# ScalarE in place of VectorE for the normalised rows between two MLPs

## The chip, the core and the metric

The kernel runs on one core of a Trainium2 chip. A core has a matrix engine (TensorE, PE in the rows), a vector engine (VectorE, DVE), an engine for functions of one input (ScalarE, ACT), a general engine (GpSimd, POOL) and a queue that issues transfers (SyncE, SP). Each works through its own instructions in a fixed order and waits on semaphores for the others. The metric is the device time of one execution in microseconds, as a median over runs.

## What is computed

A decayed linear attention is followed by a token and channel MLP, then by a Fourier mixing, a normalisation of each row and a second channel MLP. The change lies in the normalisation:

```python
X = np.fft.fft(np.fft.fft(x, axis=1), axis=2)
u = x + np.real(X).astype(np.float32)
mu = np.mean(u, axis=-1, keepdims=True)
var = np.mean((u - mu) ** 2, axis=-1, keepdims=True)
un = (u - mu) / np.sqrt(var + 1e-06)
ch = np.maximum(un @ w_ch1, 0.0) @ w_ch2
return (u + ch).astype(np.float32)
```

There are two batches of 768 rows with 512 features; the first MLP has 1536 hidden features, the second 2048. Everything is float32. A product in float32 is made of three products of a rounded high part and a low part (`mm3`, L118 to L120), so each operand is split first: ACT rounds the high part and DVE or POOL subtracts it.

## The kernel before

A batch's 768 rows are six tiles of 128 rows (`u3[b][:, r, :]`, r from 0 to 5), each 128 partitions by 512 features. `fourier_rows` writes them: TensorE transposes the input into a bank `pu` (L860), DVE adds the transform (L867, L868). `norm(b, rows)` takes rows 0 to 3 at once, and later rows 4 and 5: DVE makes the statistics of each row (L882, L883), ACT the square root (L885), DVE the reciprocal with one correction step (L886 to L889, 128x4 or 128x2 numbers), and then DVE writes each normalised tile `unf_b_r`, (u - mean) * rs, with the mean and rs as one number per partition (L893). `norm_out` has TensorE transpose `unf` into a bank `pn` (L902), ACT round it (L908) and DVE subtract (L909), which makes `un`, the input of the second MLP.

This work is woven into the MLPs' own. While batch 0's rows are normalised, the first MLP of batch 1 is still running, and the transform of batch 1 begins: `fourier_ab` makes two sums `abt` at a time, one on DVE and one on POOL (L698), ACT and DVE split them into `ab` (L113, L114), and `fourier_d` multiplies them into banks `pq`.. `first` makes a block of hidden features: TensorE fills a bank `ph`, ACT makes the rounded positive part `hid` (L486), DVE the low part (L487). `second` multiplies `hid` into the accumulators `ac`. `convert` prepares one weight tile: a transfer brings the raw weights, ACT rounds them into `w_a` or `w_b` (L252), POOL subtracts (L253).

The banks `pu`, `pn`, `pq`, `pm` share two buffers (`x_bank`), so a product into one of them waits until ACT or DVE has emptied the one before the last. The tiles `unf`, `abt`, `z`, `at` share nine buffers (`temp`), the raw weights three.

A list by step numbers (`WHEN`, `TURNS`) sets the order of TensorE's and SP's instructions as the code is written. The instructions of ACT, DVE and POOL are put in order by the scheduler that builds the program; each engine's order is then fixed. In the names below, `hid_0_1_1_9` is the hidden block 9 of the first MLP, batch 1, half 1; `w_a_1_2` the weight tile 2 of the second MLP; `abt_1_0_0_1` the sum for batch 1, half 0, kind 0, made by POOL.

Of the kernel before, what the change touches and what calls it, by code (L numbers as in the profile page):

```python
# [14 lines left out]
AF = mybir.ActivationFunctionType  # L15
ALU = mybir.AluOpType
# [44 lines left out]
def body(ctx: ExitStack, tc: tile.TileContext, qkv, kT, lam, w_tok1, w_tok2,  # L61
         w_ch1, w_ch2, m_ch1, m_ch2, dft, dft_x, out, scratch, singles):
    nc = tc.nc
# [14 lines left out]
    ts = nc.vector.tensor_scalar  # L78
    stt = nc.vector.scalar_tensor_tensor
# [28 lines left out]
    def temp(w, n, dt=F32):  # L108
        return t_p.tile([P, 2 * NQ + 2], dt, tag="t", name=n)[:, :w]
# [150 lines left out]
    def convert(n=1, among=()):  # L260

        among = list(among)
        for _ in range(n):
            if at_["part"] < at_["word"] and (jobs[at_["part"]][0] == "ahead" or room(jobs[at_["part"]][1])):
                stage_part()
            if at_["word"] < at_["abs"] and at_["word"] < at_["part"] + 1:
                for op in word_ops():
                    op()
                    if among:
                        among.pop(0)()  # L270
            while at_["load"] < at_["word"] + BUFS["raw"] and len(raws) < BUFS["raw"] and load_next():
                pass
            if at_["abs"] < at_["word"] + 1:
                stage_abs()
        for op in among:
            op()
# [213 lines left out]
    u3 = {}  # L490
# [381 lines left out]
    def norm(b, rows):  # L872

        n = len(rows)
        r0 = rows[0]
        st = sm_p.tile([P, n, 6], F32, tag="bn", name=f"bn_{b}_{r0}", bufs=2)
        mv = sm_p.tile([P, n, 2], F32, tag="mv", name=f"mv_{b}_{r0}", bufs=2)
        var = sm_p.tile([P, n], F32, tag="var", name=f"var_{b}_{r0}", bufs=2)
        rs = sm_p.tile([P, n], F32, tag="rs", name=f"rs_{b}_{r0}", bufs=2)
        t1 = sm_p.tile([P, n], F32, tag="t1", name=f"t1_{b}_{r0}", bufs=2)  # L880
        for i, r in enumerate(rows):
            nc.vector.bn_stats(out=st[:, i, :], in_=u3[b][:, r, :])  # L882
            nc.vector.bn_aggr(out=mv[:, i, :], in_=st[:, i, :])  # L883
        ts(out=var, in0=mv[:, :, 1], scalar1=EPS, scalar2=None, op0=ALU.add)
        nc.scalar.activation(t1, var, AF.Sqrt)  # L885
        ops = [lambda: nc.vector.reciprocal(rs, t1),  # L886
               lambda: tt(out=t1, in0=rs, in1=rs, op=ALU.mult),
               lambda: stt(out=t1, in0=t1, scalar=-0.5, in1=var, op0=ALU.mult, op1=ALU.mult),
               lambda: stt(out=rs, in0=t1, scalar=1.5, in1=rs, op0=ALU.add, op1=ALU.mult)]  # L889
        convert(1, ops)  # L890
        for i, r in enumerate(rows):
            un = temp(DM, f"unf_{b}_{r}")
            ts(out=un, in0=u3[b][:, r, :], scalar1=mv[:, i, 0:1], scalar2=rs[:, i:i + 1],  # L893
               op0=ALU.subtract, op1=ALU.mult)
            uns[b, r] = un

    def norm_out(b, rows):
# [41 lines left out]
    for b in range(B):  # L939
        for h, (fn, *args) in zip(WHEN[b], (  # L940
                (fourier_ab, b, 0, 0), (fourier_ab, b, 0, 1), (fourier_d, b, 0, 0), (fourier_d, b, 0, 1),
                (fourier_ab, b, 1, 0), (fourier_ab, b, 1, 1), (fourier_d, b, 1, 0), (fourier_d, b, 1, 1),
                (fourier_sums, b, 0), (fourier_sums, b, 1), (fourier_y, b, 0), (fourier_y, b, 1),
                (fourier_gather, b), (fourier_columns, b, 0), (fourier_rows, b, 0), (fourier_columns, b, 1),
                (fourier_rows, b, 1), (fourier_mid, b), (fourier_columns, b, 2), (norm, b, (0, 1, 2, 3)),
                (fourier_rows, b, 2), (norm_out, b, (0, 1)), (norm_out, b, (2, 3)), (norm, b, (4, 5)),
                (norm_out, b, (4, 5)))):
            side.setdefault(h, []).append((fn, args))
# [198 lines left out]
```

## Time and profile before

| | |
|---|---|
| median of three runs | 619.23 us (619.03 to 619.75) |
| the profiled execution | 619.02 us, of which the span is 617.2 us |
| busy in the span: TensorE, VectorE, ScalarE, GpSimd | 589.6, 438.3, 235.0, 144.4 us |
| granted TensorE clock | 1.00 of 2.4 GHz throughout |

TensorE is busy nearly all the time, so the places where it waits are what is to be read. The timelines of the engines show these, each row with the idle time ahead of it and the instruction that ended it. A wait for several things is put down to the one that came last by the profile. The tables of `norm` for batch 0 lie at 301 to 323 us, those for batch 1 at 377 to 402.

### The profile page before, as it was taken

The numbers are of one execution on the slowest core, as the hardware profiler recorded it, in microseconds if no ns is written. First come the engines' busy times: TensorE is split into PE (matmuls) and PEld (weight loads), VectorE is DVE, ScalarE is ACT, GpSimd is POOL, SyncE is SP. The second block draws the span as 40 slices with busy tenths as digits, with TensorE's granted clock in tenths as the row PEclk, the third lists the DMA queues.
The fourth block names the chain that finished last, engine by engine and source line by source line (L and its number), as shares of the span: only waits on it lengthen the run. The fifth ranks groups of instructions, "written<-read, shape, count | busy, mean of one in ns | idle before, by whom it ended". The sixth has DMA issues, their size and how long they took to land. (4 is left out here: it accounts for less than half of the span.)

```text
span 617.2 us, 9630 instructions
## 1 busy us (share of the span) xinstructions
PE 589.6 (96%) x3704; PEld 545.2 (88%) x3704; DVE 438.3 (71%) x823; ACT 235.0 (38%) x480; POOL 144.4 (23%) x119
## 2 busy tenths in 40 slices
PE   8789999999999999999999999999989998999997
PEld 7777799899899999999989899878878887888896
DVE  6798998893876448638796875895798688343435
ACT  2575763532423323234454441343443333211110
POOL 5253224220400220201364110033402332300000
PEclk9999999999999999999999999999999999999999
DMA  8966335333387256100232001002405342000005
GB/s 282 406 236 225 110 102 176 103 113 110 109 268 241 69 189 219 67 1 1 60 95 70 19 1 34 18 18 81 125 0 175 116 120 87 0 1 0 1 2 204
DMA packets 24638, 65.58 MB, mean 106 GB/s; under 512 B 2824, under 2 KB 3984, under 8 KB 24592
## 3 DMA queue, kind: packets, MB, share of 16 engines
q1 hardware_dynamic: 24304, 64.83, 31.7%
q8 instruction: 29, 0.48, 0.3%
q10 hardware_dynamic: 288, 0.14, 0.1%
q14 instruction: 17, 0.14, 0.1%
HBM read 54.99 MB, written 9.97 MB: 105 GB/s over the span
## 5 line engine op out<-in xcount | busy, mean ns | idle before, releaser
L120 PE MATMUL ac<-w_b,hid 128*128 128x512 f32 x192 | 75.9, 396 | 0.3 <-DVE hid L487 0.3
L119 PE MATMUL ac<-w_b,hid 128*128 128x512 f32 x192 | 75.7, 394 | 0.0
L118 PE MATMUL ac<-w_b,hid 128*128 128x512 f32 x192 | 74.9, 390 | 0.0
L487 DVE SCALAR_TENSOR_TENSOR hid<-ph,hid 128x384 fp32r<-128x384 f32 x68 | 37.5, 551 | 50.6 <-ACT hid L486 50.6
L119 PE MATMUL ac<-hid,w_b 128*128 128x384 f32 x192 | 65.2, 339 | 2.9 <-DVE hid L487 2.7
L118 PE MATMUL ac<-hid,w_b 128*128 128x384 f32 x192 | 64.8, 337 | 0.3 <-ACT hid L486 0.3
L118 PE MATMUL ph<-uh,w_a 128*128 128x384 f32 x192 | 64.7, 337 | 0.0
L120 PE MATMUL ph<-uh,w_a 128*128 128x384 f32 x192 | 64.3, 335 | 0.0
L120 PE MATMUL ac<-hid,w_b 128*128 128x384 f32 x192 | 64.2, 335 | 0.0
L119 PE MATMUL ph<-uh,w_a 128*128 128x384 f32 x192 | 64.2, 334 | 0.0
L486 ACT ACTIVATE hid<-ph 128x384 fp32r<-128x384 f32 x68 | 33.1, 487 | 79.8 <-PE ph L120 79.8
L253 POOL TENSOR_TENSOR w_a<-m_a,w_a 128x512 fp32r<-128x512 f32 x18 | 26.2, 1454 | 104.3 <-ACT w_a L252 104.3
L120 PEld LDWEIGHTS ac<-w_b,hid 128*128 128x128 f32 x192 | 36.0, 187 | 8.4 <-DVE hid L487 0.8
L119 PEld LDWEIGHTS ac<-w_b,hid 128*128 128x128 f32 x192 | 36.0, 188 | 6.1
L118 PEld LDWEIGHTS ac<-w_b,hid 128*128 128x128 f32 x192 | 36.1, 188 | 5.8
L119 PEld LDWEIGHTS ac<-hid,w_b 128*128 128x128 f32 x192 | 36.0, 188 | 5.5 <-DVE hid L487 5.5
L253 POOL TENSOR_TENSOR w_b<-m_b,w_b 128x512 fp32r<-128x512 f32 x18 | 25.4, 1413 | 59.4 <-ACT w_b L252 44.5
L118 PEld LDWEIGHTS ac<-hid,w_b 128*128 128x128 f32 x192 | 36.1, 188 | 1.0 <-ACT hid L486 0.6
L118 PEld LDWEIGHTS ph<-uh,w_a 128*128 128x128 f32 x192 | 36.1, 188 | 0.3 <-issue 0.2
L119 PEld LDWEIGHTS ph<-uh,w_a 128*128 128x128 f32 x192 | 36.1, 188 | 0.1
L120 PEld LDWEIGHTS ac<-hid,w_b 128*128 128x128 f32 x192 | 36.0, 188 | 0.0
L120 PEld LDWEIGHTS ph<-uh,w_a 128*128 128x128 f32 x192 | 36.0, 188 | 0.0
(453 smaller groups left out, 1464.2 us busy)
## 6 DMA issues: line engine op xcount, KB each, us to landing
qkv<-qkv SPq DMA_DIRECT2D x7, 768.0 KB, 9.1
single_scratch<-m_a SPq DMA_DIRECT2D x16, 256.0 KB, 4.1
qkv<-qkv SPq DMA_DIRECT2D x10, 384.0 KB, 5.9
kp<-kT SPq DMA_DIRECT2D x8, 384.0 KB, 6.8
out<-u SPq DMA_DIRECT2D x11, 256.0 KB, 2.0
single_scratch<-m_b SPq DMA_DIRECT2D x10, 256.0 KB, 4.8
raw_t_0d<-w_tok SPq DMA_DIRECT2D x2, 384.0 KB, 9.9
raw_t_1d<-w_tok SPq DMA_DIRECT2D x2, 384.0 KB, 4.2
```

The lines of the kernel that those rows point to most:

```text
L118: nc.tensor.matmul(ps, wt[0], xt[0], start=first, stop=False, **kw)
L119: nc.tensor.matmul(ps, wt[0], xt[1], start=False, stop=False, **kw)
L120: nc.tensor.matmul(ps, wt[1], xt[0], start=False, stop=last, **kw)
L253: nc.gpsimd.tensor_tensor(out=t[:, 1, :n], in0=src, in1=f32(t[:, 0, :n]), op=ALU.subtract)
L486: nc.scalar.activation(hi, ps, AF.Relu)
L487: stt(out=lo, in0=ps, scalar=0.0, in1=f32(hi), op0=ALU.max, op1=ALU.subtract)
```

## The change

Each group gets one more small DVE instruction, t1 = -mean * rs (L890 of the new kernel). The normalised tile is then written by ACT as rs * u + t1, with rs as a scale and t1 as a bias per partition (L894); L893 on DVE is gone.

```diff
-               lambda: stt(out=rs, in0=t1, scalar=1.5, in1=rs, op0=ALU.add, op1=ALU.mult)]
+               lambda: stt(out=rs, in0=t1, scalar=1.5, in1=rs, op0=ALU.add, op1=ALU.mult),
+               lambda: stt(out=t1, in0=mv[:, :, 0], scalar=-1.0, in1=rs, op0=ALU.mult, op1=ALU.mult)]
         convert(1, ops)
         for i, r in enumerate(rows):
             un = temp(DM, f"unf_{b}_{r}")
-            ts(out=un, in0=u3[b][:, r, :], scalar1=mv[:, i, 0:1], scalar2=rs[:, i:i + 1],
-               op0=ALU.subtract, op1=ALU.mult)
+            nc.scalar.activation(un, u3[b][:, r, :], AF.Identity, scale=rs[:, i:i + 1], bias=t1[:, i:i + 1])
```

The scheduler puts other instructions into another order as well. On ACT, at rows 0 to 3 of batch 0, this stands before:

```order
L849 ACTIVATE z_0_2_3246<-at_0_2_3244 128x2x2
L252 ACTIVATE w_a_1_2_3361<-raw_a_1_2s_3281 128x512
L486 ACTIVATE hid_0_1_1_9_3275<-ph_0_1_1_9_3262 128x384
L252 ACTIVATE w_b_1_2_3368<-raw_b_1_2s_3286 128x512
L252 ACTIVATE w_a_1_3_3457<-raw_a_1_3s_3364 128x512
L908 ACTIVATE un_0_0_3335<-pn_0_0_3330 128x4x128
```

In the new program ACT has there:

```order
L849 ACTIVATE z_0_2_3246<-at_0_2_3244 128x2x2
L894 ACTIVATE unf_0_0_3311<-u3_0_3115,t1_0_0_3292,rs_0_0_3291 128x512
L894 ACTIVATE unf_0_1_3313<-u3_0_3115,t1_0_0_3292,rs_0_0_3291 128x512
L894 ACTIVATE unf_0_2_3315<-u3_0_3115,t1_0_0_3292,rs_0_0_3291 128x512
L894 ACTIVATE unf_0_3_3317<-u3_0_3115,t1_0_0_3292,rs_0_0_3291 128x512
L486 ACTIVATE hid_0_1_1_9_3275<-ph_0_1_1_9_3262 128x384
L252 ACTIVATE w_a_1_2_3362<-raw_a_1_2s_3281 128x512
L252 ACTIVATE w_b_1_2_3369<-raw_b_1_2s_3286 128x512
L252 ACTIVATE w_a_1_3_3458<-raw_a_1_3s_3365 128x512
L908 ACTIVATE un_0_0_3336<-pn_0_0_3331 128x4x128
```

The four new instructions stand behind L849, and the rounding of the weights `w_a_1_2` has moved from ahead of `hid_0_1_1_9` to behind it.

On POOL, at the same place, before:

```order
L253 TENSOR_TENSOR w_b_1_1_3303<-raw_b_1_1s_3228,w_b_1_1_3303 128x512
L253 TENSOR_TENSOR w_a_1_2_3361<-raw_a_1_2s_3281,w_a_1_2_3361 128x512
L698 TENSOR_TENSOR abt_1_0_0_1_3391<-xT_1_178 128x384
L253 TENSOR_TENSOR w_b_1_2_3368<-raw_b_1_2s_3286,w_b_1_2_3368 128x512
L253 TENSOR_TENSOR w_a_1_3_3457<-raw_a_1_3s_3364,w_a_1_3_3457 128x512
L698 TENSOR_TENSOR abt_1_0_1_1_3399<-xT_1_178 128x384
```

In the new program POOL has there:

```order
L253 TENSOR_TENSOR w_b_1_1_3303<-raw_b_1_1s_3228,w_b_1_1_3303 128x512
L698 TENSOR_TENSOR abt_1_0_0_1_3392<-xT_1_178 128x384
L253 TENSOR_TENSOR w_a_1_2_3362<-raw_a_1_2s_3281,w_a_1_2_3362 128x512
L253 TENSOR_TENSOR w_b_1_2_3369<-raw_b_1_2s_3286,w_b_1_2_3369 128x512
L253 TENSOR_TENSOR w_a_1_3_3458<-raw_a_1_3s_3365,w_a_1_3_3458 128x512
L698 TENSOR_TENSOR abt_1_0_1_1_3400<-xT_1_178 128x384
```

The first `abt` has moved ahead of `w_a_1_2`. It waits there for L849 on ACT, the last reader of the tile whose buffer it takes; before, it waited for the DVE instructions ahead.

On ACT at rows 0 to 3 of batch 1 the new program has these rows; before, the four L894 were not among them:

```order
L842 ACTIVATE at_1_2_4070<-pm_1_2_0_4056 128x258
L252 ACTIVATE w_a_1_7_4239<-raw_a_1_7s_4093 128x512
L894 ACTIVATE unf_1_0_4100<-u3_1_3862,t1_1_0_4080,rs_1_0_4079 128x512
L849 ACTIVATE z_1_2_4072<-at_1_2_4070 128x2x2
L894 ACTIVATE unf_1_1_4102<-u3_1_3862,t1_1_0_4080,rs_1_0_4079 128x512
L894 ACTIVATE unf_1_2_4104<-u3_1_3862,t1_1_0_4080,rs_1_0_4079 128x512
L894 ACTIVATE unf_1_3_4106<-u3_1_3862,t1_1_0_4080,rs_1_0_4079 128x512
L908 ACTIVATE un_1_0_4122<-pn_1_0_4117 128x4x128
```

One of them stands ahead of L849 and three behind it; all four stand ahead of L908. The orders of TensorE and SP are the same in both programs. On DVE the other instructions keep their order but for L890 and a swap of two neighbours behind rows 4 and 5 of batch 1.

## Rows read from the trace of the kernel before

**Rows 1.** Page, busy time: engine, us, share of the span, instructions.
```profile
PE 589.6 (96%) x3704; PEld 545.2 (88%) x3704; DVE 438.3 (71%) x823; ACT 235.0 (38%) x480; POOL 144.4 (23%) x119
```

**Rows 2.** Timeline of TensorE: start, length, operation, count, idle ahead and its releaser.
```profile
312.27 1.03 PE L902 MATMUL pn<-ident,unf 128*128 128x128 f32 x8
...
315.97 0.63 PE L860 MATMUL pu<-ident,g 128*128 128x128 f32 x4 [0.57 <-DVE un L909]
...
320.82 0.36 PE L118 MATMUL pq<-w_dft,ab 128*128 128x256 f32 x1 [0.77 <-DVE mv L883]
```

**Rows 3.** Timeline of DVE in the same stretch.
```profile
306.06 1.19 DVE L884 TENSOR_SCALAR var<-mv 128x4 f32<-128x4 f32 x1
...
308.42 0.16 DVE L889 SCALAR_TENSOR_TENSOR rs<-t,rs 128x4 f32<-128x4 f32 x1
308.62 4.56 DVE L893 TENSOR_SCALAR unf<-u,mv,rs 128x512 f32<-128x512 f32 x4
...
317.75 0.54 DVE L487 SCALAR_TENSOR_TENSOR hid<-ph,hid 128x384 fp32r<-128x384 f32 x1
...
318.88 0.54 DVE L114 TENSOR_TENSOR ab<-abt,ab 128x384 fp32r<-128x384 f32 x1
...
320.27 0.41 DVE L868 TENSOR_TENSOR u<-pu,z 128x256 f32<-128x256 f32 x1
```

**Rows 4.** Timeline of ACT in the same stretch.
```profile
308.00 0.21 ACT L849 ACTIVATE z<-at 128x4 f32<-128x4 f32 x1 [0.51 <-DVE rs L886]
308.31 0.63 ACT L252 ACTIVATE w_a<-raw_a_2s 128x512 fp32r<-128x512 f32 x1
310.39 0.49 ACT L486 ACTIVATE hid<-ph 128x384 fp32r<-128x384 f32 x1 [1.45 <-PE ph L120]
310.78 0.62 ACT L252 ACTIVATE w_b<-raw_b_2s 128x512 fp32r<-128x512 f32 x1
...
316.12 0.52 ACT L113 ACTIVATE ab<-abt 128x384 fp32r<-128x384 f32 x1 [0.34 <-POOL abt L698]
316.55 0.47 ACT L486 ACTIVATE hid<-ph 128x384 fp32r<-128x384 f32 x1
```

**Rows 5.** Timeline of POOL in the same stretch.
```profile
305.93 1.29 POOL L253 TENSOR_TENSOR w_b<-raw_b_1s,w_b 128x512 fp32r<-128x512 f32 x1 [2.20 <-ACT w_b L252]
309.02 1.29 POOL L253 TENSOR_TENSOR w_a<-raw_a_2s,w_a 128x512 fp32r<-128x512 f32 x1 [1.79 <-ACT w_a L252]
310.27 1.20 POOL L698 TENSOR_TENSOR abt<-xT 128x384 f32<-128x384 f32 x1
...
313.18 1.63 POOL L253 TENSOR_TENSOR w_a<-raw_a_3s,w_a 128x512 fp32r<-128x512 f32 x1 [0.28 <-ACT w_a L252]
314.77 1.32 POOL L698 TENSOR_TENSOR abt<-xT 128x384 f32<-128x384 f32 x1
317.62 1.36 POOL L253 TENSOR_TENSOR w_b<-raw_b_3s,w_b 128x512 fp32r<-128x512 f32 x1 [1.53 <-ACT w_b L252]
```

**Rows 6.** Groups of ACT instructions by form: count, busy us, mean ns, idle ahead.
```profile
L252 ACT ACTIVATE w_a<-m_a 128x512 fp32r<-128x512 f32 x18 | 11.3, 626 | 13.7 <-DVE m_a L226 12.7 <-PE h L120 0.7 <-PE ht L120 0.3
...
L401 ACT ACTIVATE qkv<-qkv,att 128x320 f32<-128x320 f32 x16 | 8.3, 553 | 13.5 <-DMA qkv<-qkv 5.4 <-DVE att L338 5.0 <-DMA att<-pw_scratch 3.0
L113 ACT ACTIVATE ab<-abt 128x384 fp32r<-128x384 f32 x16 | 7.8, 519 | 7.4 <-POOL abt L698 6.9 <-DVE abt L698 0.4
```

**Rows 7.** Timeline of TensorE at rows 0 to 3 of batch 1.
```profile
388.63 1.09 PE L902 MATMUL pn<-ident,unf 128*128 128x128 f32 x8 [0.40 <-DVE unf L893]
```

**Rows 8.** Timelines of ACT, DVE and POOL at rows 0 to 3 of batch 1.
```profile
386.19 0.63 ACT L252 ACTIVATE w_a<-raw_a_7s 128x512 fp32r<-128x512 f32 x1 [0.33 <-PE pm L120]
...
389.29 1.09 ACT L908 ACTIVATE un<-pn 128x512 fp32r<-128x512 f32 x2 [1.97 <-PE pn L902]
...
386.93 2.91 DVE L893 TENSOR_SCALAR unf<-u,mv,rs 128x512 f32<-128x512 f32 x4
...
386.90 1.29 POOL L253 TENSOR_TENSOR w_a<-raw_a_7s,w_a 128x512 fp32r<-128x512 f32 x1 [14.98 <-ACT w_a L252]
```

## The prediction

> **What bounds the kernel now.** I read the page's busy times first, then TensorE's timeline in the stretch of the normalisation, then the timelines of VectorE (DVE), ScalarE (ACT) and GpSimd (POOL) over the same stretch. TensorE is busy for 96% of the span [rows 1]: a microsecond saved elsewhere is worth something only where TensorE waits, and a microsecond added costs something only where TensorE is made to wait. Two places have such waits beside the moved lines. For batch 0, TensorE waits 0.57 us before the transposes into `pu` at 315.97 and 0.77 us before the second product into `pq` at 320.82 [rows 2]. The last is named as a wait for a DVE instruction of that moment; what it needs is the bank that L868 empties, from 320.27 for 0.41 us [rows 3], 0.14 us before TensorE goes on. For batch 1, TensorE waits 0.40 us for the normalised rows themselves at 388.63 [rows 7].
>
> The DVE instructions that the change takes away are stretched where POOL works beside them: four L893 take 4.56 us from 308.62 [rows 3], while POOL runs from 309.02 almost without a gap [rows 5]. In batch 1, with one POOL instruction beside them, four take 2.91 us [rows 8].
>
> **The change, part by part.** It takes twelve DVE instructions away, four groups of 4, 2, 4 and 2, adds one small DVE instruction (L890) to each group, and puts twelve ACT instructions (L894) into ACT's queue. The order of TensorE and of SP stays. ACT's order and POOL's order do not.
>
> *Price of one L894.* No ACT instruction of the trace has a scale and a bias per partition. With constants, 128x512 takes 0.626 us and 128x384 0.519 [rows 6], so 0.84 ns an element and 0.466 us for 320 elements. L401, with a scale per partition over 320 elements, takes 0.553 [rows 6], 0.087 more. Two such operands give 0.626 + 2 x 0.087 = 0.80 us. ACT instructions in a row start about 0.10 us before the one ahead ends (0.49 us from 310.39, the next at 310.78 [rows 4]), so one L894 each 0.71 us; the bounds are 0.53 (the operands cost nothing) and 0.80 (no overlap). I take 0.71, being worked out from the one row that has such an operand. The Trainium skill, ScalarE: Activation LUTs, in What ACT_TABLE_LOAD costs, gives 186 ns plus 0.833 ns an element plus about 93 ns for each pointer operand, by which one would take 0.80 us as well; the trace agrees for one operand, and no run here yet shows two. The functions' table is loaded once at the start in both programs.
>
> *Batch 0, rows 0 to 3.* This is where the time is decided.
>
> 1. POOL's `abt` (the input of the row transform) now stands ahead of `w_a_1_2` and waits only for L849, which ends at 308.21 [rows 4]. With the 0.08 us that POOL needs after an ACT instruction (308.94 to 309.02 [rows 4, 5]) it starts at 308.29. L889 comes on DVE at 308.42 [rows 3], reads two tiles from SBUF, and meets it. L884, as small, was held from 306.06 for 1.19 us until POOL's instruction of 305.93 had ended [rows 3, 5]. So L889 ends with POOL's 1.20 us [rows 5], at 309.5, L890 0.2 later, and the first L894 starts at 309.75. Without that meeting it would start at 308.85.
> 2. Four L894 take 4 x 0.71 = 2.84 us: `hid_0_1_1_9` starts at 312.6 instead of 310.39. In the old order `w_a_1_2` went ahead of it at 308.31; now it comes 0.39 us behind, at 313.0, ends 0.63 later at 313.6 [rows 4], and POOL begins its half at 313.7 instead of 309.02.
> 3. POOL then has four instructions before the second `abt` is there: `w_a_1_2`, `w_b_1_2`, `w_a_1_3`, `abt`. The four from 310.27 to 316.09 took 5.54 us without their one gap of 0.28 [rows 5], with DVE working against them. Alone they would take 3 x 1.25 + 1.20 = 4.95. DVE has four two-input instructions in this time again (`abt`, three L114), so I take 5.54: the second `abt` ends at 319.2 instead of 316.09.
> 4. ACT waits for that `abt` (L113 at 316.12), and `hid_0_1_1_10` stands behind it (316.55 [rows 4]); now 319.7, 3.1 us later. On DVE that tile's L487 stands ahead of L867, L868, L114, BN_STATS, L867 and L868 for the rows 4 and 5, and TensorE's second `pq` waits for the last of them. From the start of `hid_0_1_1_10` on ACT to this `pq` it is 4.27 us now [rows 2, 4]. DVE was about 0.7 us late there (L487 at 317.75 [rows 3]), which goes. In its place L114 meets POOL's `w_b_1_3`, which in the old run was nearly done (317.62 for 1.36, L114 at 318.88 [rows 3, 5]); that gives some 0.5 back. I take 4.05: `pq` starts at 323.75 instead of 320.82, **2.9 us later**.
>
> The 0.57 us at `pu` may stay or go: TensorE comes to `pq` early in both cases and waits there. The transposes of the new rows are not late: TensorE comes to them at 312.27 [rows 2], and the first L894 ends at 310.6. The raw weights that wait for POOL to free their buffers (from `raw_b_1_3` on, in SP's queue) are asked for some 5 us later; their readers on ACT stand behind the same delay, so I cost that at nothing, and at up to 1 us if one of them lands late. Bounds of the 2.9: 0.3 below (no meeting at L889, 0.53 each, POOL alone, no meeting at L114: 2.9 - 0.9 - 0.7 - 0.6 - 0.4), 4.0 above.
>
> *Batch 1, rows 0 to 3.* `w_a_1_7` starts on ACT at 386.19 [rows 8], so the first L894 at 386.7, done by 387.5; no stretch by POOL, which held L893 from 386.93 [rows 8]. TensorE finds it at 388.1 or so and saves its 0.40 us [rows 7] and some 0.2 of starting anew (an estimate: matmuls in a row overlap, and after a wait the first does not). But three more L894 and L849 stand ahead of L908, which moves from 389.29 [rows 8] to about 389.7, and the banks come free later for the next transposes: 0.3 of it remains. **0.3 us gained**, bounds 0 and 0.6.
>
> *Rows 4 and 5 of both batches.* Two L894 each, begun where ACT waited for TensorE, and read by transposes that follow a block of the MLP's products later; nothing. DVE's freed time (about 10 us in all) is idle time, as DVE waits there for ACT and TensorE.
>
> *Sum.* The profiled execution took 619.02 us, 617.2 of span and 1.8 around it. 619.02 + 2.9 - 0.3 = 621.6. The median of the three runs is 0.21 above this execution, so 621.8 against 619.23, 0.4% slower.
>
> **The rivals.**
>
> *DVE was the limit, and it is freed: faster.* If POOL's chain didn't reach `hid_0_1_1_10` late, the waits at `pu`, `pq` and `pn` would all go: 0.57 + 0.77 + 0.40 [rows 2, 7] and about 0.2 for each new start, 2.3 us, so 617.0. For it: all three waits name DVE, and four L893 took 4.56 us beside a busy POOL against 2.91 in batch 1 [rows 3, 8]. Against it: it decides only if the second `abt` ends before about 315.5, and POOL's four instructions cannot begin before `w_a_1_2` is rounded on ACT, behind four L894. The Trainium skill, SBUF — State Buffer, in Who interferes with whom, says that ACT never waits for another engine's port while such a DVE instruction is shut out for the whole of a GpSimd instruction; by that rule alone the move is a gain. The stretched L893 agree with it.
>
> *L889 doesn't meet POOL.* Then everything from step 2 is 0.9 us earlier: 620.9.
>
> *The delay is hidden.* L894 at 0.53 us, no meeting at L889 and POOL alone: 0.3 to 0.7 late, 0.3 gained, 619.4, no change. It decides if the second `abt` ends by about 317.
>
> *Worse.* The four POOL instructions each held by a DVE instruction for 0.3 us more, or a late raw weight: 623 or above.
>
> **How the numbers follow.** Forecast, 621.8: 0.55. L889 free, 620.9: 0.17. Hidden, 619.4: 0.15. Faster, 617.0: 0.07. Worse, 623 and above: 0.06. A difference of 0.2%, 1.24 us, is about what a measurement of this kernel can tell from no change, so slower begins at 620.5: the forecast, the worse case and two thirds of the second rival, 0.73. No change: the hidden case and the rest, 0.20. Faster 0.07. The range takes in the hidden case and the bounds of the POOL chain: 619.3 to 623.0.
>
> **What would show it.** In the new profile: L894 near 0.80 us, four in about 2.9. L889 of batch 0 near 1.2 us instead of 0.16. POOL idle for some 4 us between `abt` and `w_a_1_2`. `hid_0_1_1_10` on ACT behind a wait for POOL's `abt`. TensorE waiting some 2 us or more before the first `pq` and again before the second, about 3.6 us more in this stretch than before it loses to `pu`; no wait at batch 1's first `pn`. I am wrong if POOL's four instructions start before 312, if `pq` has no longer wait than now, or if a wait after 330 shrinks by as much, since I take every later wait to move along with TensorE.

## The result and the profile after the change

The changed kernel takes 623.40 us, median of six runs (622.23 to 625.67), against 619.59 us for the kernel before in the same comparison: a ratio of 1.0062, 95% interval 1.0041 to 1.0084. It is slower, as forecast, but by 3.8 us instead of the forecast 2.6, and its time lies 0.4 us above the range. The profiled execution took 623.28 us with a span of 621.48, 4.2 us more than the 617.25 of the kernel before.

The page's busy line of the changed kernel (engine, us, share of the span, instructions):

```profile
PE 593.5 (95%) x3704; PEld 549.7 (88%) x3704; DVE 429.6 (69%) x815; ACT 243.4 (39%) x492; POOL 145.2 (23%) x119
```

DVE has 8.7 us less work and ACT 8.4 more, as meant. TensorE has the same 3704 matmuls and is busy for 3.9 us longer. A matmul's work has not changed, so the same matmuls ran more slowly somewhere. A part of it lies near 30 us, where the clock and the waits differ from one execution to the next and nothing was moved. The rest shows in its timeline at rows 0 to 5 of batch 0 (start, length, operation, count, idle ahead and its releaser):

```profile
311.87 1.04 PE L902 MATMUL pn<-ident,unf 128*128 128x128 f32 x8
...
315.43 0.63 PE L860 MATMUL pu<-ident,g 128*128 128x128 f32 x4 [0.41 <-DVE un L909]
...
321.15 0.42 PE L118 MATMUL pq<-w_dft,ab 128*128 128x256 f32 x1 [2.40 <-DVE u L868]
...
323.44 0.55 PE L118 MATMUL pq<-w_dft,ab 128*128 128x256 f32 x1 [0.81 <-DVE mv L883]
323.79 0.42 PE L119 MATMUL pq<-w_dft,ab 128*128 128x256 f32 x1
...
326.14 0.52 PE L118 MATMUL ph<-uh,w_a 128*128 128x384 f32 x1
...
328.27 0.34 PE L119 MATMUL ph<-uh,w_a 128*128 128x384 f32 x1
...
329.17 1.03 PE L902 MATMUL pn<-ident,unf 128*128 128x128 f32 x8
```

Two things answer to [rows 2]. There are waits of 2.40 and 0.81 us ahead of the two `pq`, where before there was one of 0.77. And the matmuls behind the first wait are longer: a `pq` takes 0.41 to 0.42 us and a `ph` 0.52, until from 328.27 on a `ph` takes 0.34 again. The windows of the same stretch, 1 us each (busy us and count for each engine, then the granted clock):

```profile
core 0: us, PE busy (x) PEld busy (x) DVE busy (x) ACT busy (x) POOL busy (x), PEclk, DMA share, GB/s
...
319.00:320.00 1.00, 0.00 (x0) 0.00 (x0) 0.45 (x2) 1.00 (x3) 0.00 (x0) 1.00 0.57 203
320.00:321.00 1.00, 0.00 (x0) 0.00 (x0) 1.00 (x4) 0.50 (x2) 0.65 (x1) 1.00 0.00 0
321.00:322.00 1.00, 0.85 (x4) 0.88 (x5) 1.00 (x3) 1.00 (x3) 0.62 (x1) 0.65 0.00 0
322.00:323.00 1.00, 0.63 (x3) 0.34 (x2) 1.00 (x4) 0.34 (x2) 0.91 (x1) 0.50 0.42 88
...
327.00:328.00 1.00, 1.00 (x4) 1.00 (x4) 0.00 (x0) 1.00 (x2) 0.00 (x0) 0.50 0.00 0
328.00:329.00 1.00, 1.00 (x7) 1.00 (x7) 0.00 (x0) 0.17 (x1) 0.00 (x0) 0.94 0.00 0
```

TensorE stands still for two windows. The granted clock falls in the window after them to 0.65, and is 0.50 in the six from 322 to 328, the lower of its two levels, 1.2 GHz; in the next it is nearly back. In the kernel before its windows from 310 to 330 all show 1.00.

One execution is profiled of each kernel, but the mean granted clock is known of many more. In the six of the changed kernel it is 0.989 to 0.994, 0.992 on the mean; in 32 of the kernel before, of another comparison, 0.991 to 1.000, on the mean 0.996, and only six of them have 1.000, as the profiled one has. So the kernel before loses time to the clock too in most of its executions. One minus the clock, times the span, comes to about 4.9 us for the changed kernel and 2.5 for the one before (an estimate): the change adds some 2.4 us of it, beside 2.13 in C of the profiled one.

To see how much each of the two is worth, I cut TensorE's timeline at instructions that both programs have: from the first `pn` of batch 0 to the first `pq` (A), to the second `pq` (B), to the `pn` of rows 2 and 3 (C). The clock's part is C, since nothing in C waits: 323.44 to 329.17, 5.73 us. The rest of the program is cut at the `pn` in the same way.

| us | A | B | C | A to C | to the `pn` of rows 4 and 5 | to batch 1's first `pn` | its next | to rows 4 and 5 | to the end |
|---|---|---|---|---|---|---|---|---|---|
| before | 6.86 | 1.69 | 3.60 | 12.15 | 13.46 | 50.75 | 3.00 | 12.22 | 213.40 |
| after | 9.28 | 2.29 | 5.73 | 17.30 | 13.45 | 50.23 | 2.98 | 12.39 | 213.26 |
| difference | +2.42 | +0.60 | +2.13 | +5.15 | -0.01 | -0.52 | -0.02 | +0.17 | -0.14 |

Together with the first `pn`, which comes 0.40 us earlier (311.87 against 312.27; POOL's `w_b_1_1`, ahead of the moved instructions, is as early, 305.53 against 305.93, so the change has no part in it), this is the 4.2 us. Batch 0 costs 3.02 us of waits (A and B) and 2.13 us of clock (C), and batch 1 gives 0.52 back and takes 0.17 of it away again.

The waits come about through ACT, POOL and DVE, whose timelines of the changed kernel follow in this order:

```profile
309.21 2.93 ACT L894 ACTIVATE unf<-u,t,rs 128x512 f32<-128x512 f32 x4 [1.41 <-DVE t L890]
312.05 0.47 ACT L486 ACTIVATE hid<-ph 128x384 fp32r<-128x384 f32 x1
312.42 0.62 ACT L252 ACTIVATE w_a<-raw_a_2s 128x512 fp32r<-128x512 f32 x1
...
318.85 0.52 ACT L113 ACTIVATE ab<-abt 128x384 fp32r<-128x384 f32 x1 [2.57 <-POOL abt L698]
319.28 0.47 ACT L486 ACTIVATE hid<-ph 128x384 fp32r<-128x384 f32 x1
```

```profile
307.95 1.01 POOL L698 TENSOR_TENSOR abt<-xT 128x384 f32<-128x384 f32 x1 [1.13 <-PE ac L120]
313.12 1.61 POOL L253 TENSOR_TENSOR w_a<-raw_a_2s,w_a 128x512 fp32r<-128x512 f32 x1 [4.16 <-ACT w_a L252]
...
317.49 1.33 POOL L698 TENSOR_TENSOR abt<-xT 128x384 f32<-128x384 f32 x1
```

```profile
308.02 0.96 DVE L889 SCALAR_TENSOR_TENSOR rs<-t,rs 128x4 f32<-128x4 f32 x1
...
315.80 3.43 DVE L114 TENSOR_TENSOR ab<-abt,ab 128x384 fp32r<-128x384 f32 x3
319.78 0.56 DVE L487 SCALAR_TENSOR_TENSOR hid<-ph,hid 128x384 fp32r<-128x384 f32 x1 [0.55 <-ACT hid L486]
...
320.59 0.41 DVE L868 TENSOR_TENSOR u<-pu,z 128x256 f32<-128x256 f32 x1
320.92 1.11 DVE L114 TENSOR_TENSOR ab<-abt,ab 128x384 fp32r<-128x384 f32 x1
...
322.89 0.41 DVE L868 TENSOR_TENSOR u<-pu,z 128x256 f32<-128x256 f32 x1
```

L889 takes 0.96 us instead of 0.16 [rows 3], as POOL's `abt` runs beside it from 307.95. Four L894 take 2.93 us, and `hid` and the weights `w_a_1_2` stand behind them. POOL waits 4.16 us for these weights, then its second `abt`, the fourth instruction from there, ends at 318.82. ACT waits 2.57 us for that, DVE 0.55 us for the `hid` behind it, and TensorE for L868 at 320.59 and again for L868 at 322.89.

### The profile page after: what moved, and what is told of

Read it like the earlier page. It is cut to its first block, busy times and chain, and to the rows that moved or that the text cites. A ratio compares the mean times of both kernels' runs of the same rounds, so it can differ in the third digit from the quotient of the medians.

```text
span 621.5 us, 9630 instructions
## 1 busy us (share of the span) xinstructions
PE 593.5 (95%) x3704; PEld 549.7 (88%) x3704; DVE 429.6 (69%) x815; ACT 243.4 (39%) x492; POOL 145.2 (23%) x119
## 5 line engine op out<-in xcount | busy, mean ns | idle before, releaser
L487 DVE SCALAR_TENSOR_TENSOR hid<-ph,hid 128x384 fp32r<-128x384 f32 x68 | 37.6, 553 | 56.1 <-ACT hid L486 56.1
```

Of the source, the lines that this page charges most:

```text
L487: stt(out=lo, in0=ps, scalar=0.0, in1=f32(hi), op0=ALU.max, op1=ALU.subtract)
```

## Experiments

Each kernel's edit is given against the changed kernel unless its text says otherwise. The waits and cuts of a row are those of one profiled execution. The ratios of e1 to e10 are to runs of the kernel before on the same chip, which had medians of 617.9 to 618.3 us there. The cuts A, B and C repeat from kernel to kernel to some hundredths of a us where nothing in them was touched (C is 3.59 to 3.63 wherever the clock stays up), while the ratios have intervals of 0.2 to 0.4% to each side; so the reasons below rest on the cuts, and the ratios are there to see whether the cuts carry to the whole time.

| kernel | waits of TensorE at `pu`, first `pq`, second `pq` | A | B | C | A to C | ratio [95%] |
|---|---|---|---|---|---|---|
| before | 0.57, none, 0.77 | 6.86 | 1.69 | 3.60 | 12.15 | |
| after | 0.41, 2.40, 0.81 | 9.28 | 2.29 | 5.73 | 17.30 | 1.0062 [1.0041, 1.0084] |
| e1 | 0.55, none, 0.78 | 6.88 | 1.67 | 3.59 | 12.14 | 1.0009 [0.9987, 1.0032] |
| e2 | 0.88, 0.39, 0.66 | 7.82 | 1.60 | 3.59 | 13.01 | 1.0023 [1.0000, 1.0045] |
| e8 | none, 2.37, 1.40 | 8.58 | 2.35 | 5.13 | 16.06 | 1.0052 [1.0021, 1.0083] |
| e9 | 0.42, 1.75, 0.78 | 8.64 | 1.72 | 5.06 | 15.42 | 1.0035 [1.0014, 1.0056] |
| e3 | 0.44, 0.20, 0.69 | 9.29 | 2.30 | 7.91 | 19.50 | 1.0126 [1.0090, 1.0162] |
| e5 | 0.43, 0.21, 0.69 | 9.29 | 2.29 | 3.59 | 15.17 | 1.0030 [1.0008, 1.0053] |
| e4 | 0.55, 2.96, 0.47 | 9.99 | 1.43 | 5.17 | 16.59 | 1.0074 [1.0054, 1.0094] |
| e6 | 0.55, 1.50, 0.47 | 8.53 | 1.42 | 3.63 | 13.58 | 1.0023 [1.0001, 1.0045] |
| e7 | none, none, 0.72 | 5.97 | 1.59 | 3.60 | 11.16 | 0.9987 [0.9967, 1.0006] |
| e10 | none, none, 0.71 | 5.97 | 1.58 | 3.60 | 11.15 | 0.9985 [0.9957, 1.0013] |

**Which group costs the time (e1).** Rows 0 to 3 of batch 0 are made by DVE again; the other three groups stay on ACT.

```diff
+        if b == 0 and n == 4:
+            ops.pop()
...
-            nc.scalar.activation(un, u3[b][:, r, :], AF.Identity, scale=rs[:, i:i + 1], bias=t1[:, i:i + 1])
+            if b == 0 and n == 4:
+                ts(out=un, in0=u3[b][:, r, :], scalar1=mv[:, i, 0:1], scalar2=rs[:, i:i + 1],
+                   op0=ALU.subtract, op1=ALU.mult)
+            else:
+                nc.scalar.activation(un, u3[b][:, r, :], AF.Identity, scale=rs[:, i:i + 1], bias=t1[:, i:i + 1])
```

> The changed kernel, with the four normalised tiles of rows 0 to 3 of batch 0 written by DVE again; the other eight stay on ACT. Theory (the loss comes from this group alone: four L894 stand ahead of w_a_1_2 on ACT, POOL's second abt is late, TensorE waits before pq, and its clock then falls): orders of ACT and POOL at that place are those of before, so the 2.4 us wait before pq goes, the clock stays at 1.00 there, and batch 1's gain remains: 619.0, 0.4 below before. Rival (ACT's extra time costs wherever it stands): eight of twelve L894 remain, so two thirds of the 3.8 us loss, 622.

A to C is 12.14 us, that of the kernel before, with the same waits and no fall of the clock. Batch 1 keeps its 0.48 us less (50.27 against 50.75) and its 0.19 more (12.41 against 12.22). So the first group alone costs the 5.15 us, and batch 1's group on ACT is a gain of 0.3. The ratio, 1.0009 with 0.2% to each side, shows no loss any more, and can't show so small a gain.

**Through which engine (e2, e8, e9).** In e2 the second `abt` of batch 1 is made by DVE, so that POOL's queue can't hold ACT there:

```diff
-            add = nc.gpsimd if j else nc.vector
+            add = nc.gpsimd if j and (b, c, par) != (1, 0, 1) else nc.vector
```

> The changed kernel, with one instruction moved: the second abt of batch 1, half 0 (abt_1_0_1_1) is made by DVE instead of POOL. All twelve L894 stay. Theory: hid_0_1_1_10 on ACT no longer waits for POOL (2.57 us in the changed kernel); TensorE's wait before the first pq falls from 2.4 to under 0.7 us, that before the second to about 1, the clock does not fall: 619.7, between 619.2 and 620.5. Rival (the L894 themselves, or L889 held by POOL, are what TensorE waits for): the waits and the time stay, 623.4.

The first `pq` comes 1.46 us earlier than in the changed kernel (A 7.82) although DVE has more to do, the clock stays at 1.00, and A to C is 13.01: 4.29 of the 5.15 us are gone. So most of the price came through POOL's queue. That it was the `abt` alone is not shown by this: in e2 one of the three L114 on DVE has also moved from ahead of L487 to behind it. 0.86 us remains.

In e8 it is the first `abt` that DVE makes, which takes away what L889 met (the same edit with `(1, 0, 0)` for `(1, 0, 1)`):

> The changed kernel, with the first abt (abt_1_0_0_1) made by DVE, so that POOL stands still when L889 comes. Theory: L889 takes 0.16 us instead of 0.96, the four L894, w_a_1_2, POOL's four instructions and the first pq are 0.8 earlier, and TensorE's wait there is 1.6 instead of 2.4: a stretch of 16.5 if the clock falls behind it, 14.4 if not. Rival (the hold of L889 is hidden): the wait stays 2.4 and the stretch 17.3.

DVE in e8:

```profile
307.00 0.17 DVE L889 SCALAR_TENSOR_TENSOR rs<-t,rs 128x4 f32<-128x4 f32 x1
```

L889 takes 0.17 us again. The first `pq` comes 0.70 us earlier (A 8.58), of the 0.80 us that L889 had lost, but TensorE, which no longer waits at `pu`, comes to it 0.67 us earlier too and waits 2.37 and 1.40 us all the same. The clock falls (C 5.13), and A to C is 16.06. The meeting at L889 is real and worth 0.7 us up to the first `pq`; without it the delay behind the four L894 still reaches TensorE.

In e9 one pair of neighbours is swapped in POOL's queue and nothing else moves: the second `abt` stands ahead of `w_a_1_3`.

```diff
-        nc.gpsimd.tensor_tensor(out=t[:, 1, :n], in0=src, in1=f32(t[:, 0, :n]), op=ALU.subtract)
+        with tc.issue_after(abt_ins[1, 0, 1, 1]) if key == ("a", 1, 3) else contextlib.nullcontext():
+            nc.gpsimd.tensor_tensor(out=t[:, 1, :n], in0=src, in1=f32(t[:, 0, :n]), op=ALU.subtract)
...
```

> The changed kernel with one swap in POOL's queue: the second abt of batch 1 stands ahead of the subtraction for w_a_1_3 instead of behind it; every other order on every engine is the same. Theory (POOL's queue makes the waits and the waits make the clock fall): abt ends 1.5 to 1.6 us earlier, at about 317.2; hid_10 starts on ACT at about 317.7; TensorE waits about 0.8 us before the first pq instead of 2.40 and about 0.8 before the second; the granted clock stays at 1.00 from 320 to 330 and the pq matmuls at 0.28 us; from the first pn to the third pn about 17.30 - 1.6 - 2.1 = 13.6 us, median about 3.7 us below the changed kernel. Rival (the clock falls for another reason, such as ACT's work at this place): the waits shrink by 1.6 and the clock falls all the same: 15.7 us. Rival (POOL's order doesn't matter since ACT or DVE holds hid_10): 17.3 us.

Neither the theory's 13.6 us nor a rival's figure came out: A to C is 15.42. DVE of the kernel before, then DVE and TensorE in e9 (line numbers are higher there: L115 is L114 and L491 is L487 of the changed kernel):

```profile
316.35 1.48 DVE L114 TENSOR_TENSOR ab<-abt,ab 128x384 fp32r<-128x384 f32 x3
```

```profile
315.66 3.43 DVE L115 TENSOR_TENSOR ab<-abt,ab 128x384 fp32r<-128x384 f32 x3
319.01 0.54 DVE L491 SCALAR_TENSOR_TENSOR hid<-ph,hid 128x384 fp32r<-128x384 f32 x1
```

```profile
320.37 0.36 PE L119 MATMUL pq<-w_dft,ab 128*128 128x256 f32 x1 [1.75 <-DVE u L873]
...
322.09 0.55 PE L119 MATMUL pq<-w_dft,ab 128*128 128x256 f32 x1 [0.78 <-DVE mv L888]
```

ACT has `hid` done by 318.05, as expected, but DVE isn't there to take it: its three L114 take 3.43 us beside a POOL that runs without a pause, where they took 1.48 before, and L491 starts at 319.01, only 0.63 us earlier in the program than in the changed kernel (7.28 us behind the first `pn` instead of 7.91). My expectation had left out that this second chain was only 0.55 us shorter than the first. With the waits of 1.75 and 0.78 the clock falls all the same in the profiled execution, from about 322.0 on (C 5.06). It doesn't in each: three of the ten executions of e9 have a mean granted clock of 1.000.

The cut A repeats this in each of these kernels, in which TensorE waits at the first `pq`: it comes 1.35 to 1.37 us after DVE's L487 (after 319.78 and 321.15, e2 316.73 and 318.08, e8 318.07 and 319.43, e9 319.01 and 320.37). So what sets the end of the first wait is whichever is later at L487, ACT's `hid` behind POOL's `abt`, or the L114 that POOL holds on DVE.

**What the clock is worth (e3, e5).** Here TensorE doesn't stand still in the wait: 20 transposes of the identity matrix ahead of the first `pq` and 6 ahead of the second go into a bank that nobody reads.

```diff
+            if (b, c, par) == (1, 0, 0) and t < 2:
+                fill = ph_bank(f"fill_{t}") if t == 0 else fill
+                for _ in range((20, 6)[t]):
+                    nc.tensor.transpose(fill[:, :P], ident, ident)
             ps = x_bank(f"pq_{b}_{c}_{par}_{t}")
```

> The changed kernel, with 20 transposes of the identity put on TensorE ahead of the first pq and 6 ahead of the second, into a bank of the hidden blocks that nobody reads; nothing else waits less. Theory (2.1 of the loss are the clock, which fell to 1.2 GHz after TensorE had stood still): the first pq starts as late as in the changed kernel, the granted clock stays at 1.00 at 320 to 330 us, and the time is 2.1 lower, 621.3. Rival (the clock fell for another reason than the idle stretch, or costs nothing on this path): 623.4, or above it by what the transposes take.

In e3 the clock stayed up over both `pq` (0.28 us each), but the scheduler had put L885 and one of the later L894 on ACT ahead of the emptying of `pq`. TensorE waited for this 2.51 us at a third `pq`, and the clock fell behind that: A to C 19.50. Up to the second `pq` it reads as the theory wanted; as a whole it decides nothing. In e5 ACT's order is held to that of the changed kernel:

```diff
...
-        nc.scalar.activation(t1, var, AF.Sqrt)
+        with ExitStack() as hold:
+            if b == 0 and n == 2:
+                hold.enter_context(tc.issue_after(on_act["q", 1]))
+            nc.scalar.activation(t1, var, AF.Sqrt)
...
-            nc.scalar.activation(un, u3[b][:, r, :], AF.Identity, scale=rs[:, i:i + 1], bias=t1[:, i:i + 1])
+            with ExitStack() as hold:
+                if b == 0 and n == 2:
+                    hold.enter_context(tc.issue_after(on_act["q", 2]))
+                nc.scalar.activation(un, u3[b][:, r, :], AF.Identity, scale=rs[:, i:i + 1], bias=t1[:, i:i + 1])
...
```

> As e3 (20 and 6 transposes of the identity in TensorE's two waits ahead of pq), but with ACT's later instructions held in the changed kernel's order, since in e3 two L894 had moved ahead of the emptying of pq and made a third wait of 2.5 us. Measured on TensorE from the first pn of batch 0 to its third: 12.15 us before, 17.30 in the changed kernel. Theory (2.1 of the 5.15 are the clock, which falls because TensorE stands still): 15.2, the granted clock 1.00 at 320 to 330. Rival (the clock falls for another reason): 17.3 or more.

```profile
core 0: us, PE busy (x) PEld busy (x) DVE busy (x) ACT busy (x) POOL busy (x), PEclk, DMA share, GB/s
...
320.00:325.00 5.00, 4.31 (x31) 4.10 (x32) 4.04 (x13) 2.28 (x8) 1.75 (x2) 1.00 0.40 107
325.00:330.00 5.00, 5.00 (x37) 4.97 (x36) 1.85 (x3) 4.10 (x8) 1.53 (x2) 1.00 0.09 14
```

A and B are 9.29 and 2.29, those of the changed kernel to 0.01: the two `pq` come as late as ever. The clock is 1.00 throughout, and C is 3.59, that of the kernel before. So the lost clock is worth 2.13 us in the profiled execution, and the lateness by itself 3.02. The other executions fit this: the ratio goes from 1.0062 to 1.0030, about 2 us, though the intervals overlap, and the ten of e5 have a mean granted clock of 0.996, that of the kernel before.

**Whether lateness alone lowers the clock (e4, e6).** Both are the kernel before, with nothing on ACT, in which the emptying of `pu` on DVE is made late by four (e4) or two (e6) more BN_STATS, whose result isn't used:

```diff
+            if b == 0 and r == 4:
+                late = sm_p.tile([P, 6], F32, name="late")
+                for _ in range(4):
+                    nc.vector.bn_stats(out=late, in_=px)
```

> The kernel before, with four more BN_STATS on DVE that read the bank pu of row tile 4 and write a tile that nobody reads; they hold this bank for 4 x 0.62 = 2.5 us longer. No work moves to ACT. Theory: TensorE waits about 2.3 us before the first pq, as in the changed kernel, and its clock falls behind it as there: 619.5 + 2.5 + 2.1 = 624. Rival (the clock did not fall because of the wait): 2.5 later alone, 622.

> The kernel before with two more BN_STATS on DVE that hold the bank pu of row tile 4 for 1.2 us, half of e4's dose, which made a wait of 2.96 us and a stretch of 16.59. Theory, if the clock falls only behind the longer wait: 12.15 + 1.4 = 13.5, clock 1.00. If it falls behind any wait: 12.15 + 1.4 + 2 = 15.6. If the wait alone costs and the clock is an accident, e4's 4.4 halves: 14.3.

TensorE in e4, and then in e6:

```profile
320.30 0.35 PE L118 MATMUL pq<-w_dft,ab 128*128 128x256 f32 x1 [2.96 <-DVE u L872]
...
321.73 0.38 PE L118 MATMUL pq<-w_dft,ab 128*128 128x256 f32 x1 [0.47 <-ACT q L716]
...
322.29 0.42 PE L118 MATMUL pq<-w_dft,ab 128*128 128x256 f32 x1
```

```profile
318.15 0.36 PE L118 MATMUL pq<-w_dft,ab 128*128 128x256 f32 x1 [1.50 <-DVE u L872]
...
319.57 0.38 PE L118 MATMUL pq<-w_dft,ab 128*128 128x256 f32 x1 [0.47 <-ACT q L716]
319.79 0.28 PE L119 MATMUL pq<-w_dft,ab 128*128 128x256 f32 x1
```

With a wait of 2.96 us the clock falls in the kernel before too, from about 322.0 on, and C is 5.17. With 1.50 and 0.47 us it does not in the profiled execution, and C is 3.63. L894 isn't needed for the fall; a late `pq` can bring it about.

**A kernel without the delay (e7, e10).** Only rows 0 and 1 are normalised ahead of `hid`; the L894 of rows 2 and 3 are written behind the start of the transposes, where ACT has room. In e7 this is done for batch 0, in e10 for both batches.

```diff
-            un = temp(DM, f"unf_{b}_{r}")
-            nc.scalar.activation(un, u3[b][:, r, :], AF.Identity, scale=rs[:, i:i + 1], bias=t1[:, i:i + 1])
-            uns[b, r] = un
+            def normed(r=r, i=i):
+                un = temp(DM, f"unf_{b}_{r}")
+                nc.scalar.activation(un, u3[b][:, r, :], AF.Identity, scale=rs[:, i:i + 1], bias=t1[:, i:i + 1])
+                return un
+            uns[b, r] = normed if b == 0 and r in (2, 3) else normed()
...
+        for r in rows:
+            if callable(uns[b, r]):
+                uns[b, r] = uns[b, r]()
```

> The changed kernel, with the L894 of rows 2 and 3 of batch 0 written down later, where they are transposed. Two instead of four stand ahead of w_a_1_2 on ACT, and since the buffers turn otherwise, POOL's second abt comes ahead of w_a_1_2 too. Theory: hid_0_1_1_10 no longer waits for POOL, no wait of more than 1 us before pq, no fall of the clock; the stretch from the first to the third pn of batch 0 takes 11.4 to 12.4 us, the whole about 0.3 to 1 below before: ratio to before 0.9985 to 0.9995. Rival (ACT is short of time for the twelve L894 wherever they stand): the stretch stays above 14.

> As e7_two_rows_later (two of the four L894 of rows 0 to 3 written behind the transposes' start) and in batch 1 as well as in batch 0. Theory: batch 0 as in e7, 11.2 us from the first pn to the third, no clock fall; in batch 1 the two L894 that are left ahead of L849 and L908 let L908 start some 1 us earlier than in the changed kernel, but TensorE waits there for nothing, so nothing more is gained: from the first to the third pn of batch 1 2.98 to 3.0 us, median within 0.5 us of e7, 0.1 to 0.4% below the kernel before. Rival (batch 1's later L908 held TensorE's banks in the changed kernel): another 0.2 to 0.5 us less between the third pn and the first pn of batch 1.

ACT in e7 (L895 is L894 of the changed kernel):

```profile
309.55 1.53 ACT L895 ACTIVATE unf<-u,t,rs 128x512 f32<-128x512 f32 x2 [1.34 <-DVE t L890]
310.98 0.62 ACT L252 ACTIVATE w_a<-raw_a_2s 128x512 fp32r<-128x512 f32 x1
311.50 0.47 ACT L486 ACTIVATE hid<-ph 128x384 fp32r<-128x384 f32 x1
...
315.62 0.49 ACT L486 ACTIVATE hid<-ph 128x384 fp32r<-128x384 f32 x1
```

Two L894 end at 311.08 and `hid` starts at 311.50. `w_a_1_2` is rounded ahead of it again, POOL keeps up (both `abt` now stand ahead of the weights, as the buffers come free in another order), and ACT's second `hid` at 315.62 waits for nothing. The waits at `pu` and at the first `pq` are gone, and A to C is 11.16 us, 0.99 less than before and 0.24 below the lower end of what was expected. 0.29 us of it is lost again on the way to the `pn` of rows 4 and 5 (13.75 against 13.46 us); I have not traced that. e10 repeats A to C at 11.15 and takes back the loss in batch 1: 12.21 us between its second and third pair of `pn`, where the kernels with four L894 there have 12.38 to 12.41 and those with DVE's L893 12.21 to 12.22. That is the rival's mechanism, in a later stretch than the one it named and at the lower end of its size; the theory's "nothing more is gained" fell, if only by 0.2 us. By its cuts up to batch 1's rows 4 and 5 e10 is 1.20 us shorter than the kernel before; its median is 0.9 us lower, with an interval from 0.43% faster to 0.13% slower, so the whole time doesn't show a gain for certain.

## Why the prediction was right in its sign and short in its size

**The chain, steps 1 to 4: right.** With its 0.40 us earlier start added, the changed kernel's rows stand beside the forecast thus: first L894 309.61 (309.75 forecast), `hid` 312.45 (312.6), `w_a_1_2` 312.82 (313.0), POOL's half 313.52 (313.7), end of the second `abt` 319.22 (319.2), ACT's second `hid` 319.68 (319.7), second `pq` 323.84 (323.75). L889 met POOL, with 0.96 us instead of the 1.2 taken. DVE's L487 was no longer late, and L114 at 320.92 was held to 1.11 us, 0.57 more than before, where 0.5 was taken. The sum of these steps was 2.9; A and B measured 3.02, and e5, with the clock kept up, shows the same.

**Price of L894: right.** The group of all twelve (count, busy us, mean ns):

```profile
L894 ACT ACTIVATE unf<-u,t,rs 128x512 f32<-128x512 f32 x12 | 9.0, 804 | 3.1 <-DVE t L890 3.1
```

0.80 us was forecast for one and 0.71 for one in a row, 2.84 for four; four took 2.93.

**What failed: the sum has no term for TensorE's clock.** It put "2.9 us late" on the path as 2.9 us. I forecast that TensorE would stand still for 2 us or more ahead of the first `pq` and shortly after again, and priced that at its length. Behind the wait the clock was at 1.2 GHz for about 7 us, and the matmuls of C took 2.13 us more. With it the sum is 619.02 + 2.9 + 2.1 - 0.3, and 0.21 for the median: 623.9, against 623.40 measured; the 0.40 us by which the profiled execution came to its first `pn` earlier is about the rest. No rival had this mechanism either; "worse, 623 and above" named other reasons, with 0.06.

The trace of before had a row that seems to speak against such a term, and could have been weighed: in the stage that follows the second MLP, TensorE waits as long as this and goes on at full clock:

```profile
451.15 0.44 PE L118 MATMUL pb<-tops,w_s 128*128 128x384 f32 x1 [2.18 <-DVE u L614]
451.43 0.34 PE L119 MATMUL pb<-tops,w_s 128*128 128x384 f32 x1
```

2.18 us of standing still, the `pb` behind it 0.34 us each, the granted clock 1.00 as in all of this execution. But it is one execution. In e6, which changes nothing at this place, the same instruction comes after the same wait, and the clock falls to 0.50:

```profile
449.92 0.49 PE L118 MATMUL pb<-tops,w_s 128*128 128x384 f32 x1 [2.18 <-DVE u L614]
450.20 0.52 PE L119 MATMUL pb<-tops,w_s 128*128 128x384 f32 x1
```

It also falls behind this `pb` in e7, e8 and e10 (waits of 2.08, 2.18 and 2.08 us), and not in the changed kernel, e1 and e2 (2.17, 2.18 and 2.04). So behind the same wait of about 2 us the clock falls in some executions and stays up in others. A price of nothing beyond its length was one bound and should have stood as such. For the other bound the trace of before has no row, as its granted clock is 1.000 on the mean; what a fall costs is seen only now, a `pq` every 0.21 us instead of 0.12 and a `ph` every 0.32 instead of 0.17, for 6.8 us in the changed kernel and for 3.4 in e4, e8 and e9, where C grew by about 1.5 instead of 2.1. Which of the two stretches the other executions of the changed kernel had is not shown. The Trainium skill, TensorE: Matmul & The Clock Gate, in HAM oscillation — how this bites in real kernels, describes repeated waits of TensorE for transfers, of some 3 to 5 us each, behind which the matmuls that follow start at the lower clock. The waits here were shorter, 2.40 us in the trace of after and 2.96 in e4, and had the same behind them; the rows at 451.15 show one that had not. A rival with this mechanism was open to me.

**Batch 1: right.** The wait of 0.40 at the first `pn` is gone, with 0.12 for starting anew (0.52), and a part is given back as L908 comes later: 0.17, inside the transposes of the next pair. 0.3 was forecast, 0.35 measured. ACT and TensorE of the changed kernel there:

```profile
392.32 2.21 ACT L894 ACTIVATE unf<-u,t,rs 128x512 f32<-128x512 f32 x3
394.43 1.06 ACT L908 ACTIVATE un<-pn 128x512 fp32r<-128x512 f32 x2
```

```profile
392.85 1.03 PE L902 MATMUL pn<-ident,unf 128*128 128x128 f32 x8
...
395.83 1.21 PE L902 MATMUL pn<-ident,unf 128*128 128x128 f32 x8
```

L908 waits for no one but stands behind four L894, and the eight transposes from 395.83 take 1.21 us, where those of the pair ahead take 1.03, and where nothing holds them 1.03 is what eight take.

**The rivals.** *DVE is freed, faster*: its mechanism is there but not in this order of the work. In e7, where POOL's chain isn't late, the waits at `pu` and at the first `pq` are gone, and A to C falls by 1.0 us; 2.3 us was its price, and e10 comes to 1.2. *L889 free*: e8 shows 0.70 us up to the first `pq` for it where 0.9 was named, and the total stays well above the kernel before. *Hidden*: not so; in e9 even an `abt` 1.6 us earlier leaves 1.75 us of wait, since the L114 on DVE are late as well, which the prediction had not seen.

**The checks that it named.** L894 near 0.80, L889 longer, POOL idle for 4.16 us, ACT behind `abt`, no wait at batch 1's first `pn`: all there. One was worded badly: "about 3.6 us more in this stretch than before it loses to `pu`". The three waits are 3.62 us together, but those of before were 1.34, so they grew by 2.28. The rest of the 3.02 is the six matmuls of the first `pq`, which ran at half clock already (1.48 us instead of 0.92, in time that would otherwise have been wait), and some 0.2 of starting anew.

## What to carry to other kernels

An engine with room on average can still hold up the one that has none: the twelve instructions fit ACT's idle time in total, but four in a row delayed what stood behind them in its queue, from there a chain on POOL, and so TensorE. Spread over the places where the engine waits, as in e10, the same instructions cost nothing. A wait that is put on TensorE has two prices, its length and, in some executions, the slower matmuls behind it (here 1.5 to 2.1 us behind waits of about 2 to 3); look at the granted clock in windows of 1 us behind the wait, and at the mean clock of every execution, as one profile shows only one of both cases. When one chain is made shorter, look which one is next: in e9 it was 0.6 us away.

## What was not expected of the hardware

- The clock fell behind waits of 2.40 and 0.81, 2.37 and 1.40, 1.75 and 0.78, 2.51 (e3), and 2.96 and 0.47 us, for a loss of 1.5 to 2.1 us beside the waits; it did not fall behind 1.50 and 0.47 (e6). Behind one and the same wait of 2.18 us (`pb`, L614 on DVE) it fell in e6 and e8 and stayed up in the kernel before and in e1. The length of a wait doesn't settle it; what does is left open.
- With transposes of an identity matrix in the wait the granted clock stayed at 1.00 over both `pq` (e3, e5), and the executions of e5 lost no more to the clock than those of the kernel before.
- Three L114 on DVE took 3.43 us beside a POOL that ran without a gap, and 1.48 in the kernel before: the delay of POOL's queue was so not only in what POOL finished late but also in what it held on DVE.
